# Windowed attention with a gated feed-forward: a third buffer for the turned probabilities, doubled high parts of q and k in DRAM, and a new table of issue points

## The chip, the cores and the metric

The kernel runs on one core of a Trainium2 chip. Times are device microseconds of one execution. The kernel before takes 1642.25 us (median of 3 runs, 1636.55 to 1642.45). TensorE is PE in the profile, its weight load PEld; VectorE is DVE, ScalarE ACT, GpSimd POOL, SyncE SP.

## What is computed

The input x has 2048 rows of 576 numbers.

```python
xn = layernorm(x)
q, k, v = split(xn @ wqkv)                    # 32 heads of 18
mask = (i - j >= 0) & (i - j < 256)           # sliding window
p = softmax(where(mask, q @ k.T * 18**-0.5, -1e9))
s = (p @ v) @ wo
g = silu(((xn @ w_gate) * (xn @ w_up)) @ w_down)   # 576 -> 4608 -> 576
out = x + s * g
```

## The kernel before

**Numbers.** Most operands are a pair of fp16 numbers, a high part and the rest times a constant (the low part); a product runs as passes high by high, high by low and low by high.

**The prologue** (to about 183 us) normalizes x, turns it, and computes v, q and k in two halves of 1024 rows. Each finished tile of q and k (tile `qp`, high part and low part) is stored to `qk_d` in DRAM by `qk_store` (L395). At its end the weights and inputs of the first up-projection are prepared (`sx`, `tf`, `tw`: sums and differences that the seven-product scheme needs).

**Slots.** Then come 72 slots. Slot 4g + c handles the g-th group of 2 x 128 feed-forward columns (18 groups) for the c-th 512 rows. A slot has 16 places. In each place PE gets some matmuls of the up-projection (L1151, 92 of 256 columns in a slot, and L1104, eight with half the rows, four of them at place 6), and everything else is put at a place: `at(slot, place, f)` runs `f` there. A place of 16 or more lies in the next slot. The table `AT` holds the places. Engines execute in order, so a place fixes an instruction's position in the queue of its engine and not its time. SP issues all DMAs in the order of the program, and a DMA that must wait holds those behind it.

**Feed-forward in a slot.** The up results are read out of PSUM by ACT (L1117) and DVE (L1121) into `gt`. The product of gate and up (`ht`, L1126, `seven_mult`) runs on POOL for the first 128 columns and on DVE for the others. `h_hi` (L994, ACT) makes the high part `hh`, `h_lo` (L999, DVE) the low part, and the down-projection (L1015) uses both in the next slot, in five pieces; DVE adds each into `acc` (L1022). In slot 3 of each group of four (3 modulo 4) and slot 0 of the next the weights for the next group are scaled and split: L184 on ACT, L187 on DVE, sums and differences L492 on POOL, `dnw` for the down-projection, whose third part is made on POOL by L592.

**Attention in slots 1 to 64.** One step handles two heads and 512 queries, as four blocks of 128 queries, i0 to i3. A step: scores (L889), masked maxima (L900, DVE), the maxima's scaling (L908, ACT), exponential and its high part (L912, L915, ACT), the low part (L921, POOL or DVE, into `pp`), one transposing DMA for each block (`pt<-pp`, L924), the product with v (`weigh`, L933, 48 matmuls in a step), and the division and store (L945, L946, L953, L960, L961, L970). Table row `p` holds the places of score, shift, exponential, turn and weigh for each block and head. The loads of k, q and v for the next step are L862, L869 and L876. `pt` has two buffers: a block's transpose can start when the block two before it has been weighed.

**The end.** In slots 68 to 70 WO is loaded, its maximum taken (`wo_amax`, through DRAM and back into all partitions, `sd_wo` and `spread`), and scaled (`wo_scale`, L1219, and `wo_split`). From about 1580 us the output projection runs (L1254).

Of the kernel before, what the change touches and what calls it, by code (L numbers as in the profile page):

```python
# [20 lines left out]
def kernel(  # L21
# [23 lines left out]
    scale = DH ** -0.5  # L45
# [14 lines left out]
    G_SC, U_SC, LO = 2.0 ** -23, 2.0 ** -13, 2.0 ** 11  # L60
# [4 lines left out]
    C_OUT = 1.0 / (XS * PROJ * WTOP * WTOP)  # L65
    LEAST, MOST = 2.0 ** -60, 2.0 ** 60

    AT = {"amax": (18, 18, 12),
           "dn": ((43, 42), (53, 57), (57, 54)),
           "down": (6, 8, 11, 14, 17),  # L70
           "end": (28, 30, 33),
           "eng": (0, 1, 0, 0, 0, 0, 0, 0, 0, 0, 1, 0, 0, 0),
           "g0": (-25, -25, -18, -5, -33, -14, -12, -10, -2),
           "h": ((15, 17), (18, 19)),
           "load": (3, 8, 10),
           "mult": {1: 3, 4: 8, 5: 1, 6: 1},
# [6 lines left out]
           "pairs": (6, 13),  # L83
           "raw": (8, 13, 15, 16, -3, -1),
           "scale": (20, 25, 35, 39),
           "sum": ((30, 36, 42, 60, 63), (38, 43, 50, 60, 62)),
# [5 lines left out]
           "t_hi": ((57, 58), (66, 69)),  # L92
           "t_lo": ((58, 59), (70, 70)),
           "u0": ((-9, -8, -5, -5), (-6, -8, -5, -3)),
           "up_hi": (37, 38, 63, 60),
           "up_lo": (42, 40, 65, 62),
           "wd": ((58, 46), (65, 65), (67, 66)),
           "wd0": ((-3, -8), (-1, -2), (-1, 7))}
# [8 lines left out]
    pro = pro_stack.enter_context(tc.tile_pool(name="pro", bufs=1))  # L107
    norm = norm_stack.enter_context(tc.tile_pool(name="norm", bufs=1, side="right"))

    qk_d = dram.tile([2, 2 * D, S], F16, name="qk_d")  # L110
    v_d = dram.tile([S, H * VW], F16, name="v_d")
    o_d = [dram.tile([512, 2 * D], F16, name=f"o_d{i}") for i in range(NCH)]

# [2 lines left out]
    XT2 = const.tile([128, S], F16, name="XT2")  # L116
# [226 lines left out]
    UW, DW, RAW, HT, GT, SC = {}, {}, {}, {}, {}, {}  # L343
# [112 lines left out]

    TF, TW, SX, XD = {}, {}, {}, {}
# [50 lines left out]
    def s_steps(c):  # L510
# [46 lines left out]
        s, m = OP.add, OP.subtract  # L557
# [55 lines left out]
    def at(slot, place, f, *a):  # L613
        todo.setdefault(slot * 16 + place, []).append((f, a))
# [53 lines left out]
    a, b = TB.pop(0)  # L668
# [94 lines left out]
    for t in range(16):  # L763
# [35 lines left out]
        for m in range(QM):  # L799
            for c in (2 * half, 2 * half + 1):  # L800
                qk_tile(UW["q", m], m, c)
                if m == 0:
                    n0 = max(128, c * 512)
# [44 lines left out]
                            fill=-3e38, base=0, channel_multiplier=1)  # L848
    QS, KS, VT, SP, SM, PP, PT, PVB, OB, O3, MX, SMT, RC = {}, {}, {}, {}, {}, {}, {}, {}, {}, {}, {}, {}, {}

    def unit(u, r1, n0, n1):
        return qk_d[0:r1 // DH, u * DH:(u + 1) * DH, n0:n1]


    def load_k(s):
        c, u = s // 16, 2 * (s % 16) + H
        k0 = max(0, c * 512 - 256)
        n = (c + 1) * 512 - k0
        KS[s] = att.tile([128, 768], F16, name="ks", bufs=2)
        for j in range(2):  # L860
            for a, r1 in ((0, 36), (36, 18)):
                nc.sync.dma_start(KS[s][64 * j + a:64 * j + a + r1, 768 - n:], unit(u + j, r1, k0, k0 + n))  # L862
# [55 lines left out]
    def turn_probs(s, j, i):  # L918
        sm, mx, n = SM.pop((s, j, i))
        pp, a = PP[s, i], n * j  # L920
        (nc.gpsimd, nc.vector)[AT["eng"][6 + 2 * i + j]].tensor_tensor(pp[:, a + 2 * n:a + 3 * n], sm, pp[:, a:a + n], op=OP.subtract)  # L921
        if j == 1:
            pt = PT[s, i] = att.tile([128, 12, 128], F16, name="pt", bufs=2)
            nc.sync.dma_start(pt[:, 0:4 * n // 128], PP.pop((s, i))[:, 0:4 * n], transpose=True)  # L924

    def weigh(s, j, i):
# [64 lines left out]

    def h_hi(sl, ft):
        h, hh = HT[sl, ft], h_ring()
        nc.scalar.activation(hh[:, 0], h, AF.Copy, scale=1.0 / LO)  # L994
        HT[sl, ft] = (h, hh)

    def h_lo(sl, ft):
        h, hh = HT[sl, ft]
        nc.vector.scalar_tensor_tensor(hh[:, 1], hh[:, 0], -LO, h, op0=OP.mult, op1=OP.add)  # L999
# [121 lines left out]
        nc.vector.scalar_tensor_tensor(seven_new(sl, name), CH[q], H_SC, x, op0=OP.mult, op1=OP.add)  # L1121

    def seven_mult(sl, f, eng):
        HT[sl, f] = f_ring("ht")
        u = SV.pop((sl, f)).rearrange("p i (k n) -> p k i n", k=2)
        eng.tensor_tensor(HT[sl, f].rearrange("p (i n) -> p i n", i=2), u[:, 0], u[:, 1], op=OP.mult)  # L1126
# [190 lines left out]
```

## Time and profile before

| | |
|---|---|
| median of 3 runs | 1642.25 us |
| the profiled execution, its own time | 1647.93 us |
| its span in the profile | 1646.2 us |
| PE, DVE, ACT, POOL busy | 96%, 77%, 64%, 53% |
| granted TensorE clock, mean | 0.992 |
| DMA moved | 206.91 MB, mean 126 GB/s |

The profiled execution is 0.35% over the median. Its span is 1.73 us shorter than its own time; that rest lies outside the instructions. In the rows, "x<-y" is what an instruction writes and reads, a bracket at the end of a timeline row is the time its engine sat idle before it and what ended that, and "SPq" is SP's queue of DMA issues.

### The profile page before, as it was taken

The numbers are of one execution on the slowest core, as the hardware profiler recorded it, in microseconds if no ns is written. First come the engines' busy times: TensorE is split into PE (matmuls) and PEld (weight loads), VectorE is DVE, ScalarE is ACT, GpSimd is POOL, SyncE is SP. The second block draws the span as 40 slices with busy tenths as digits, with TensorE's granted clock in tenths as the row PEclk, the third lists the DMA queues.
The fourth block names the chain that finished last, engine by engine and source line by source line (L and its number), as shares of the span: only waits on it lengthen the run. The fifth ranks groups of instructions, "written<-read, shape, count | busy, mean of one in ns | idle before, by whom it ended". The sixth has DMA issues, their size and how long they took to land.

```text
span 1646.2 us, 40284 instructions
## 1 busy us (share of the span) xinstructions
PE 1576.6 (96%) x15498; PEld 1106.7 (67%) x15498; DVE 1261.2 (77%) x2752; ACT 1060.2 (64%) x1817; POOL 875.5 (53%) x1100
## 2 busy tenths in 40 slices
PE   8999899999999999999999999999999999999899
PEld 5464576776767666767676667676767666677567
DVE  7536787878788878888878788887878788867555
ACT  6443576777767777777867687777777768752130
POOL 3125565747565656656565657575757475742000
PEclk9999999999999999999999999999999999999999
DMA  9572346565657777676767677777777777751228
GB/s 237 164 194 88 116 83 130 103 123 99 123 107 133 137 119 143 119 147 117 147 107 147 104 146 115 141 123 132 128 138 126 129 123 140 120 95 37 60 67 222
DMA packets 565744, 206.91 MB, mean 126 GB/s; under 512 B 506288, under 2 KB 546352, under 8 KB 565552
## 3 DMA queue, kind: packets, MB, share of 16 engines
q1 hardware_dynamic: 565552, 204.35, 63.8%
q8 instruction: 121, 1.98, 0.5%
q14 instruction: 71, 0.58, 0.1%
HBM read 76.63 MB, written 23.75 MB: 61 GB/s over the span
## 4 chain that ended last, share of the span: by engine, by line
PE 47%; DMA 11%; DVE 11%; POOL 9%; issue 9%; ACT 7%; SPq 5%; ACTq 0%; POOLq 0%; DVEq 0%
PE up L1151 20%; PE dn L1015 10%; DMA pt<-pp 7%; POOL pp L921 4%; PE s L375 3%; PE s L1015 2%; ACT pp L915 2%; PE pv L933 2%; PE s L1254 2%; SPq L924 2%; DVE upw L187 2%; DVE acc L1022 2%; PE up L1254 1%; PE up L1104 1%; PE up L375 1%
## 5 line engine op out<-in xcount | busy, mean ns | idle before, releaser
L1015 PE MATMUL dn<-dnw,hh 128*128 128x512 f16 (+1 forms) x3168 | 447.3, 286 | 9.3 <-DVE hh L999 7.2
L1151 PEld LDWEIGHTS <-tw 128*128 128x128 f16 x3456 | 317.7, 98 | 64.1 <-issue 10.2
L1015 PEld LDWEIGHTS <-hh 128*128 128x128 f16 x3456 | 222.1, 98 | 191.1 <-DVE hh L999 29.8
L1151 PEld LDWEIGHTS <-upw 128*128 128x128 f16 x3024 | 285.0, 98 | 81.9 <-issue 35.2
L1121 DVE SCALAR_TENSOR_TENSOR gt<-up,gt 128x512 f32<-128x512 f32 x360 | 247.0, 686 | 99.3 <-PE up L1104 82.7
L1022 DVE SCALAR_TENSOR_TENSOR acc<-dn,sc,acc 128x512 f32<-128x512 f32 x310 | 214.8, 693 | 112.3 <-PE dn L1015 110.5
L908 ACT ACTIVATE mx<-mx,sig 128x2 f32<-128x2 f32 x256 | 98.2, 383 | 270.3 <-DVE mx L900 270.2
L1151 PE MATMUL up<-XT,upw 128*128 128x256 f16 x2016 | 253.7, 272 | 10.4 <-ACT gt L1117 10.4
L1151 PE MATMUL up<-XT,tw 128*128 128x256 f16 x1728 | 229.4, 277 | 5.9 <-DVE gt L1121 5.9
L1151 PE MATMUL up<-sx,tw 128*128 128x256 f16 x1728 | 231.4, 273 | 2.6 <-ACT gt L1117 1.4
L933 PEld LDWEIGHTS <-pt 128*128 128x128 f16 x2880 | 115.7, 96 | 67.5 <-DMA pt<-pp 45.0
L994 ACT ACTIVATE hh<-ht 128x512 f16<-128x512 f32 x144 | 90.2, 626 | 93.4 <-POOL ht L1126 72.2
L933 PE MATMUL pv<-vt,pt 128*128 128x37 f16 x2880 | 123.4, 179 | 24.8 <-DMA pt<-pp 24.6
L1126 POOL TENSOR_TENSOR ht<-gt 128x512 f32<-128x512 f32 x72 | 92.1, 1279 | 73.2 <-DVE gt L1121 73.1
L1151 PE MATMUL up<-sx,upw 128*128 128x256 f16 x864 | 119.0, 274 | 0.0
L999 DVE SCALAR_TENSOR_TENSOR hh<-hh,ht 128x512 f16<-128x512 f16 x144 | 99.5, 710 | 1.1
L1117 ACT ACTIVATE gt<-up 128x512 f32<-128x512 f32 x144 | 83.8, 582 | 25.4 <-PE up L1104 16.1
L492 POOL TENSOR_TENSOR tf<-raw 128x256 f32<-128x256 f32 x102 | 82.1, 805 | 3.9 <-DVE sc L432 3.3
L187 DVE SCALAR_TENSOR_TENSOR upw<-raw,sc,upw 128x640 f16<-128x640 f32 x72 | 75.1, 1043 | 0.4 <-ACT upw L184 0.4
L1126 DVE TENSOR_TENSOR ht<-gt 128x512 f32<-128x512 f32 x72 | 74.6, 1036 | 0.2
L303 ACT ACTIVATE upw<-raw 128x1280 bf16<-128x1280 f32 (+1 forms) x51 | 62.8, 1232 | 12.0 <-DMA raw<-in_B_w_up_dram 11.5
L187 DVE SCALAR_TENSOR_TENSOR tw<-tf,sc,tw 128x512 f16<-128x512 f32 x68 | 52.9, 799 | 15.7 <-ACT tw L184 15.7
(1354 smaller groups left out, 2842.0 us busy)
## 6 DMA issues: line engine op xcount, KB each, us to landing
raw<-in_B_w_down_dram SPq DMA_DIRECT2D x36, 288.0 KB
qk_d<-qp SPq DMA_DIRECT2D x18, 512.0 KB
raw<-in_B_w_gate_dram SPq DMA_DIRECT2D x36, 256.0 KB
raw<-in_B_w_up_dram SPq DMA_DIRECT2D x36, 256.0 KB
vt<-v_d SPq DMA_DIRECT2D x48, 111.0 KB
ks<-qk_d SPq DMA_DIRECT2D x96, 54.0 KB
v_d<-vo SPq DMA_DIRECT2D x16, 296.0 KB
xr<-in_A_x_dram SPq DMA_DIRECT2D x16, 288.0 KB
```

The costliest lines, as they stand in the source:

```text
L187: nc.vector.scalar_tensor_tensor(w, rv, s, h, op0=OP.mult, op1=OP.subtract)
L492: nc.gpsimd.tensor_tensor(t[:, to], x0, x1, op=OP.subtract)
L908: nc.scalar.activation(mx[:, 1], mx[:, 0], AF.Identity, bias=sig[:, 2:3], scale=sig[:, 1:2])
L933: nc.tensor.matmul(PVB[s][:, j, i, :VW], pt[:, nb * j + n + n // nb * nb], VT[s][:, lo_ + n % nb, j * VW:(j + 1) * VW], start=n == 0, stop ...
L994: nc.scalar.activation(hh[:, 0], h, AF.Copy, scale=1.0 / LO)
L999: nc.vector.scalar_tensor_tensor(hh[:, 1], hh[:, 0], -LO, h, op0=OP.mult, op1=OP.add)
L1015: nc.tensor.matmul(to, a, b, start=q == 0, stop=q == len(l) - 1)
L1022: nc.vector.scalar_tensor_tensor(d, src, SC[g][:, 9:10], d, op0=OP.mult, op1=OP.add)
L1117: nc.scalar.activation(seven_new(sl, name), CH[q], AF.Copy, scale=H_SC)
L1121: nc.vector.scalar_tensor_tensor(seven_new(sl, name), CH[q], H_SC, x, op0=OP.mult, op1=OP.add)
L1126: eng.tensor_tensor(HT[sl, f].rearrange("p (i n) -> p i n", i=2), u[:, 0], u[:, 1], op=OP.mult)
L1151: nc.tensor.matmul(CH[q][:, o], a, b, start=CH["first"], stop=last and q not in (1, 2, 5), skip_group_check=q in ON)
```

## The change

It has these parts.

1. `pt` gets a third buffer. The places of turning and weighing move: the blocks are weighed at 22, 22 to 23, 26 and 28 in place of 18 to 20, 22, 25 and 27. The loads of k, q and v move from places 3, 8, 10 to 7, 10, 14.
2. `qk_d` has four planes in place of two: high, high, low, high. A store of q or k therefore takes one more DMA (two for tile 4, which holds rows of both), and a load of a head takes one DMA of 54 rows in place of two of 36 and 18.
3. The product of gate and up for the second 128 columns is written over its first operand, and one buffer holds that of the first. It is issued one place earlier; the low parts (`h_lo`) move from 18 and 19 to 20 and 21.
4. The split tail weights get a tile `wd` of their own; `xd` takes the place they had in `XT2`.
5. `eng[4]`: the third part of `dnw` is made on ACT in place of POOL.
6. WO: the maxima two places earlier, the transfer out two places earlier, its return one place later, `wo_scale` from place 0 to 6 of slot 70, the splits six places later.
7. Nearly all other places of the table move by some places, also those of the prologue's sums, of which some change between POOL and DVE.

```diff
     AT = {...
-           "eng": (0, 1, 0, 0, 0, 0, 0, 0, 0, 0, 1, 0, 0, 0),
-           "h": ((15, 17), (18, 19)),
-           "load": (3, 8, 10),
-           "p": ((6, 7, 8, 11, 18), (6, 7, 8, 11, 20), (7, 9, 10, 12, 22), (7, 9, 10, 12, 22),
-                 (13, 14, 15, 18, 25), (13, 14, 15, 19, 25), (15, 17, 18, 20, 27), (15, 17, 18, 20, 27)),
+           "eng": (0, 1, 1, 1, 1, 0, 0, 0, 0, 0, 1, 0, 0, 0),
+           "h": ((15, 17), (20, 21)),
+           "load": (7, 10, 14),
+           "p": ((6, 7, 8, 11, 22), (6, 7, 8, 12, 22), (7, 8, 10, 13, 22), (7, 9, 10, 13, 23),
+                 (13, 14, 15, 18, 26), (13, 14, 15, 19, 26), (13, 15, 20, 21, 28), (15, 17, 20, 21, 28)),
...
-    qk_d = dram.tile([2, 2 * D, S], F16, name="qk_d")
+    qk_d = dram.tile([4, 2 * D, S], F16, name="qk_d")
...
-    def f_ring(name):
-        return post.tile([128, 512], F32, name=name, bufs=4 if name == "gt" else 2)
...
-        nc.sync.dma_start(qk_d[:, m * 128:(m + 1) * 128, hs].rearrange("k r n -> r k n"), q)
+        rs = slice(m * 128, (m + 1) * 128)
+        nc.sync.dma_start(qk_d[1:3, rs, hs].rearrange("k r n -> r k n"), q)
+        for part in (0,) if m < 4 else (0, 3) if m == 4 else (3,):
+            nc.sync.dma_start(qk_d[part, rs, hs], q[:, 0])
...
     def wd_part(g, kind, i):
-        o = 1024 * (g % 2) + 512 * i + 128 * kind
-        return XT2[:, o:o + 128]
+        if g not in WD:
+            WD[g] = ring.tile([128, 2, 2, 128], F16, name="wd", bufs=1)
+        return WD[g][:, i, kind]
...
-            XD[c] = sums.tile([128, 256], F16, name=f"xd{c}")
+            XD[c] = XT2[:, 512 * c:512 * c + 256]
...
-    def unit(u, r1, n0, n1):
-        return qk_d[0:r1 // DH, u * DH:(u + 1) * DH, n0:n1]
+    def unit(u, part, n0, n1):
+        return qk_d[part:part + 3, u * DH:(u + 1) * DH, n0:n1]
...
-            for a, r1 in ((0, 36), (36, 18)):
-                nc.sync.dma_start(KS[s][64 * j + a:64 * j + a + r1, 768 - n:], unit(u + j, r1, k0, k0 + n))
+            nc.sync.dma_start(KS[s][64 * j:64 * j + 54, 768 - n:], unit(u + j, 1, k0, k0 + n))
...
-            pt = PT[s, i] = att.tile([128, 12, 128], F16, name="pt", bufs=2)
+            pt = PT[s, i] = att.tile([128, 12, 128], F16, name="pt", bufs=3)
...
-        HT[sl, f] = f_ring("ht")
         u = SV.pop((sl, f)).rearrange("p i (k n) -> p k i n", k=2)
-        eng.tensor_tensor(HT[sl, f].rearrange("p (i n) -> p i n", i=2), u[:, 0], u[:, 1], op=OP.mult)
+        HT[sl, f] = u[:, 0] if f else post.tile([128, 512], F32, name="ht", bufs=1).rearrange("p (i n) -> p i n", i=2)
+        eng.tensor_tensor(HT[sl, f], u[:, 0], u[:, 1], op=OP.mult)
...
-        at(NSLOT - 4, 2 * k + 14, wo_amax, k)
-        at(NSLOT - 2, 3 * k + 2, wo_split, k)
-    at(NSLOT - 3, 8, wo_out)
-    at(NSLOT - 3, 12, wo_in)
-    at(NSLOT - 2, 0, wo_scale)
+        at(NSLOT - 4, 2 * k + 12, wo_amax, k)
+        at(NSLOT - 2, 3 * k + 8, wo_split, k)
+    at(NSLOT - 3, 6, wo_out)
+    at(NSLOT - 3, 13, wo_in)
+    at(NSLOT - 2, 6, wo_scale)
```

Three places of the order show what the table does. The first is SP's queue from the end of slot 49 to slot 50, before: `vt`, `ks` and `qs` are loads for attention, `o_d` is a store of its result, and the four transposes are those of one step, i0 and i1 in the first row of them, then i2, then i3.

```order
L876 DMA vt<-v_d 128x6x74
L924 DMA_TRANSPOSE pt<-pp 128x12x128 x2
L970 DMA o_d_81<-ob 128x4x72
L970 DMA o_d_81<-ob 128x4x8
L924 DMA_TRANSPOSE pt<-pp 128x12x128
L862 DMA ks<-qk_d 36x1x768
L862 DMA ks<-qk_d 18x768
L862 DMA ks<-qk_d 36x1x768
L862 DMA ks<-qk_d 18x768
L924 DMA_TRANSPOSE pt<-pp 128x12x128
```

And the same part of SP's queue in the changed kernel:

```order
L923 DMA_TRANSPOSE pt<-pp 128x12x128 x2
L875 DMA vt<-v_d 128x6x74
L969 DMA o_d_81<-ob 128x4x72
L923 DMA_TRANSPOSE pt<-pp 128x12x128
L969 DMA o_d_81<-ob 128x4x8
L923 DMA_TRANSPOSE pt<-pp 128x12x128
L969 DMA o_d_81<-ob 128x4x64
L862 DMA ks<-qk_d 54x1x768 x2
L868 DMA qs<-qk_d 54x1x512 x2
```

The loads of `ks` have moved from between the transposes of i2 and i3 to behind both, and are two in place of four.

The second is POOL's queue at the end of slot 51 (3 modulo 4), before: L492 makes sums for the next group's weights, L953 to L961 finish an attention step, L1126 is the product of gate and up that ACT waits for.

```order
L921 TENSOR_TENSOR pp<-sm__18782,pp 128x384 x2
L492 TENSOR_TENSOR tf<-raw_17807,tf 128x256
L492 TENSOR_TENSOR tf<-raw_17953,tf 128x256
L953 TENSOR_TENSOR o_18885<-o_18885,rc 128x144
L960 CAST ob<-o_18885 128x4x36
L961 TENSOR_TENSOR ob<-o_18885,ob 128x4x36
L492 TENSOR_TENSOR tf<-raw_17953 128x256
L1126 TENSOR_TENSOR ht<-gt_18642 128x512
```

In the changed kernel:

```order
L920 TENSOR_TENSOR pp<-sm__18552,pp 128x384 x2
L493 TENSOR_TENSOR tf<-raw_17641,tf 128x256
L493 TENSOR_TENSOR tf<-raw_17641 128x256
L1126 TENSOR_TENSOR ht<-gt_18415 128x512
L952 TENSOR_TENSOR o_18655<-o_18655,rc 128x144
L959 CAST ob<-o_18655 128x4x36
L960 TENSOR_TENSOR ob<-o_18655,ob 128x4x36
```

The product now stands ahead of the three instructions that finish the attention step and behind one sum less.

The third is DVE's queue from the end of slot 69 into slot 70, before: L1219 to L163 are `wo_scale`, which waits for the `spread` transfer, and behind it stand the second product L1126 and the low parts L999 that the down-projection needs.

```order
L1121 SCALAR_TENSOR_TENSOR gt_24299<-up,gt_24299 128x512
L1219 TENSOR_REDUCE ps_o<-spread 128x1
L159 TENSOR_SCALAR ps_o<-ps_o 128x1
L161 TENSOR_SCALAR ps_o<-ps_o 128x1
L162 RECIPROCAL ps_o<-ps_o 128x1
L163 TENSOR_SCALAR ps_o<-ps_o 128x1
L1126 TENSOR_TENSOR ht<-gt_24299 128x512
L1022 SCALAR_TENSOR_TENSOR acc<-s,sc,acc 128x4x64
L999 SCALAR_TENSOR_TENSOR hh<-hh,ht 128x512
```

In the changed kernel:

```order
L1121 SCALAR_TENSOR_TENSOR gt_24009<-up,gt_24009 128x512
L1126 TENSOR_TENSOR gt_24009<-gt_24009 128x2x256
L1022 SCALAR_TENSOR_TENSOR acc<-s,sc,acc 128x4x64
L999 SCALAR_TENSOR_TENSOR hh<-hh,ht 128x512
L999 SCALAR_TENSOR_TENSOR hh<-hh,gt_24009 128x512
L1121 SCALAR_TENSOR_TENSOR gt_24193<-up,gt_24128 128x512
L1022 SCALAR_TENSOR_TENSOR acc<-s,sc,acc 128x512
L1219 TENSOR_REDUCE ps_o<-spread 128x1
```

Both low parts and the product now stand ahead of `wo_scale`.

More of the change, by code (lines that the diff above doesn't have):

```diff
@@ L66 @@
     LEAST, MOST = 2.0 ** -60, 2.0 ** 60
-    AT = {"amax": (18, 18, 12),
-           "dn": ((43, 42), (53, 57), (57, 54)),
+    AT = {"amax": (21, 21, 11),
+           "dn": ((44, 44), (53, 54), (52, 52)),
            "down": (6, 8, 11, 14, 17),
-           "end": (28, 30, 33),
-           "eng": (0, 1, 0, 0, 0, 0, 0, 0, 0, 0, 1, 0, 0, 0),
-           "g0": (-25, -25, -18, -5, -33, -14, -12, -10, -2),
-           "h": ((15, 17), (18, 19)),
-           "load": (3, 8, 10),
-           "mult": {1: 3, 4: 8, 5: 1, 6: 1},
[6 rows of a table removed]
+           "end": (28, 31, 35),
+           "eng": (0, 1, 1, 1, 1, 0, 0, 0, 0, 0, 1, 0, 0, 0),
+           "g0": (-21, -19, -19, -16, -30, -17, -12, -10, -7),
+           "h": ((15, 17), (20, 21)),
+           "load": (7, 10, 14),
+           "mult": {1: 11, 4: 10, 5: 1, 6: 0},
[6 rows of a table added]
            "pairs": (6, 13),
-           "raw": (8, 13, 15, 16, -3, -1),
-           "scale": (20, 25, 35, 39),
-           "sum": ((30, 36, 42, 60, 63), (38, 43, 50, 60, 62)),
+           "raw": (6, 8, 11, 13, -9, -6),
+           "scale": (22, 26, 35, 44),
+           "sum": ((29, 33, 48, 59, 66), (38, 53, 56, 61, 62)),
            "sx": ((-24, -24, -24, -23, -22, -22, -18, -18, -18, -17, -14, -13, -13, -14, -10, -10, -9),
[4 rows of a table removed]
[L92 to L98, printed above, removed]
[4 rows of a table added]
+           "t_hi": ((57, 58), (67, 69)),
+           "t_lo": ((58, 60), (70, 71)),
+           "u0": ((-8, -8, -7, -6), (-6, -8, -7, -4)),
+           "up_hi": (36, 39, 60, 59),
+           "up_lo": (41, 41, 66, 61),
+           "wd": ((55, 48), (63, 70), (67, 74)),
+           "wd0": ((-4, -8), (-1, 3), (-1, 8))}
     ctx.enter_context(tc.manual_schedule())
@@ L454, in up_lo @@
            w[:, 0:5])
-    TF, TW, SX, XD = {}, {}, {}, {}
+    TF, TW, SX, XD, WD = {}, {}, {}, {}, {}
     def wd_part(g, kind, i):
-        o = 1024 * (g % 2) + 512 * i + 128 * kind
-        return XT2[:, o:o + 128]
+        if g not in WD:
+            WD[g] = ring.tile([128, 2, 2, 128], F16, name="wd", bufs=1)
+        return WD[g][:, i, kind]
     def wd_sum(g, kind):
@@ L867, in load_q @@
         for j in range(2):
-            for a, r1 in ((0, 18), (18, 36)):
-                nc.sync.dma_start(QS[s][64 * j + a:64 * j + a + r1], unit(u + j, r1, c * 512, (c + 1) * 512))
+            nc.sync.dma_start(QS[s][64 * j:64 * j + 54], unit(u + j, 0, c * 512, (c + 1) * 512))
     def load_v(s):
@@ L993, in h_hi @@
         h, hh = HT[sl, ft], h_ring()
-        nc.scalar.activation(hh[:, 0], h, AF.Copy, scale=1.0 / LO)
+        nc.scalar.activation(hh[:, 0].rearrange("p (i n) -> p i n", i=2), h, AF.Copy, scale=1.0 / LO)
         HT[sl, ft] = (h, hh)
@@ L998, in h_lo @@
         h, hh = HT[sl, ft]
-        nc.vector.scalar_tensor_tensor(hh[:, 1], hh[:, 0], -LO, h, op0=OP.mult, op1=OP.add)
+        a, b = (hh[:, k].rearrange("p (i n) -> p i n", i=2) for k in range(2))
+        nc.vector.scalar_tensor_tensor(b, a, -LO, h, op0=OP.mult, op1=OP.add)
         HT[sl, ft] = hh
```

16 rows, old and new, of the table AT are left out of this document.

## The prediction

> **What bounds the kernel now.** I read the page first.
>
> ```profile
> span 1646.2 us, 40284 instructions
> PE 1576.6 (96%) x15498; PEld 1106.7 (67%) x15498; DVE 1261.2 (77%) x2752; ACT 1060.2 (64%) x1817; POOL 875.5 (53%) x1100
> PE 47%; DMA 11%; DVE 11%; POOL 9%; issue 9%; ACT 7%; SPq 5%; ACTq 0%; POOLq 0%; DVEq 0%
> ```
>
> PE is busy 96% of the span and idle 69.6 us. The change removes no matmul, so the gain can only come from idle time and from stretches in which PE is slow. The chain goes through DMA, DVE, POOL and ACT for 38%, so these set the pace in places. To find where, I take 48 whole slots, from place 6 of slot 17 to place 6 of slot 65; the half-row matmuls L1104 mark them in PE's timeline. The third and fourth row mark a slot in which nothing waits.
>
> ```profile
> 499.14 0.39 PE L1104 MATMUL up<-XT,upw 64*128 64x256 f16 x4
> 1399.48 0.39 PE L1104 MATMUL up<-XT,upw 64*128 64x256 f16 x4
> 1418.13 0.39 PE L1104 MATMUL up<-XT,upw 64*128 64x256 f16 x4
> 1457.77 0.39 PE L1104 MATMUL up<-XT,upw 64*128 64x256 f16 x4
> ```
>
> An undisturbed slot takes 18.65 us, so 48 would take 895.2. They take 958.6. The excess is **63.4 us**, the most that the change can win here. The busy-time windows and PE's waits of that stretch split it (waited in all, times, longest).
>
> ```profile
> 499.10:1457.80 958.70, 916.63 (x9792) 655.53 (x9792) 780.67 (x1728) 706.00 (x1178) 602.39 (x732) 0.99 0.74 130
> PE pv L933 <- DMA pt<-pp: 24.6, 26, 2.3
> PE up L1151 <- ACT gt L1117: 11.8, 13, 1.4
> PE dn L1015 <- DVE hh L999: 3.4, 12, 0.3
> PE dn L1015 <- DVE acc L1022: 2.1, 12, 0.2
> ```
>
> PE idles 42.1 us, of which the four waits are 41.9. The other 21.3 us of the excess passes while PE counts as busy. PE's timeline in slots 48 and 50, with the clock of one window, shows what that is.
>
> ```profile
> 1126.95 0.47 PE L933 MATMUL pv<-vt,pt 128*128 128x37 f16 x12 [1.97 <-DMA pt<-pp]
> 1127.26 1.76 PE L1151 MATMUL up<-XT,tw 128*128 128x256 f16 x12
> 1127.00:1131.00 4.00, 4.00 (x37) 2.44 (x38) 1.50 (x4) 0.00 (x0) 2.06 (x5) 0.66 0.96 206
> 1167.00 1.47 PE L1151 MATMUL up<-XT,tw 128*128 128x256 f16 x12
> ```
>
> After a wait of 1.97 us the granted clock is 0.66 for 4 us and twelve matmuls take 1.76 us, not 1.47. A long wait is thus paid again, 0.34 x 4.0 = 1.4 us. (The Trainium skill, "TensorE: Matmul & The Clock Gate", section "Why this matters for your kernels", sees throughput drop for PE-idle gaps over about 3 us. This trace differs: 1.97 us of idle stands right before the low clock. By that rule the slow stretches have another cause and stay; it is a rival below.) I share the 21.3 us among the waits by their idle time: 24.6 / 41.9 of it, 12.5 us, goes with the transposes. They cost **37.1 us**, the rest **26.3**.
>
> **Part 1, the transposes.** SP's timeline around the stall in slot 53, the wait at its end on PE, and a row of SP's waits:
>
> ```profile
> 1216.15 1.97 SPq L924 DMA_TRANSPOSE pt<-pp  x1
> 1218.16 2.33 SPq L862 DMA_DIRECT2D ks<-qk_d  x4
> 1220.66 2.14 SPq L924 DMA_TRANSPOSE pt<-pp  x1
> 1227.06 0.51 PE L933 MATMUL pv<-vt,pt 128*128 128x37 f16 x12 [2.02 <-DMA pt<-pp]
> SPq L924 <- PE pv L933: 31.8, 42, 1.7
> ```
>
> The first is block i2, the second i3. i3 stands behind i2, behind 2.33 us of k loads, and needs the buffer that i1 leaves; its issue ends at 1222.80 and PE can go on at 1227.06, 4.26 us later. The change takes both away: the k loads go behind i3 (and are two, so about 1.17 us of SP time), and a third buffer means that i2 needs none that this step uses and i3 only that of i0. Weighing moves later by one place for i2 and i3 (18.65 / 16 = 1.17 us) and two to four for i0, which frees nothing early but is not needed early either. In slot 53 i3 is issued 2.33 us sooner without the loads, and PE asks 1.17 later: 3.50 us against a wait of 2.02. The longest wait of all is 2.3. What could stay is the transpose that `pp` itself delays, since i3 is also turned one place later (1.17): then the margin is 2.33 against 2.3 and some remain. **Bounds**: if only the place counts, each of 26 waits (mean 0.95) loses up to 1.17, and only those over it keep a rest: by 2.3 - 1.17 at most 1.1 each, for perhaps a third of them 10 us of wait and its slow clock, so a gain of 22; with everything removed 37. I take **32**, nearer the upper end because two causes go at once.
>
> **Parts 3 and 5 and the table, slots 3 to 0 modulo 4.** The rest, 26.3 us, lies in 12 changes of group, 2.2 each. Around one of them, on POOL, ACT and PE:
>
> ```profile
> 1193.23 1.27 POOL L1126 TENSOR_TENSOR ht<-gt 128x512 f32<-128x512 f32 x1
> 1193.26 0.82 ACT L184 ACTIVATE upw<-raw,sc 128x640 f16<-128x640 f32 x1
> 1194.54 0.63 ACT L994 ACTIVATE hh<-ht 128x512 f16<-128x512 f32 x1 [0.45 <-POOL ht L1126]
> 1195.71 0.60 PE L1151 MATMUL up<-XT,upw 128*128 128x256 f16 x4 [0.95 <-ACT gt L1117]
> ```
>
> PE waits for ACT's reading L1117, which stands behind L994, which waits for the product on POOL. In the new order the product stands ahead of the finish of the attention step (L953 to L961), and ACT's weight split of 0.82 is issued earlier, with one of a quarter of that width in its place. 0.45 + about 0.4 us goes, of 0.95. But DVE has no room there:
>
> ```profile
> 1187.70:1205.90 18.20, 16.79 (x173) 11.65 (x170) 17.92 (x38) 13.94 (x26) 12.65 (x15) 1.00 0.72 141
> ```
>
> DVE (the third pair) is busy 17.92 of 18.20 us. Once ACT is in time, PE waits for DVE a little further on, at L999 or L1022, unless DVE has less to do. The split rows of the weights stay in number; some of them (one of 0.35 us, and a split of the down weights) move out of this stretch, but one maximum (L900) is issued ahead of the low parts that was behind them. I count about 0.75 us less for DVE ahead of what PE needs, and half of the 26.3 as gained: **13**, with bounds 5 (DVE takes all of what ACT gives back, and only the 3.4 + 2.1 goes) and 20 (about 1.7 a group). Moving a third of the down weights from POOL to ACT costs ACT this much:
>
> ```profile
> L592 POOL TENSOR_SCALAR dnw<-dnw 128x576 f16<-128x576 f16 x36 | 59.7, 1673 | 0.7 <-ACT dnw L184 0.7
> L184 ACT ACTIVATE dnw<-raw,sc 128x576 f16<-128x576 f32 x36 | 26.0, 767 | 0.0
> ```
>
> No row shows the operation on ACT; the nearest of its size is 767 ns, so 36 x 0.77 = 28 us for ACT, from 0 to 28 on the path. ACT is busy 64% and waits most of all for DVE's maxima, which covers it: 0. POOL gets 59.7 us back in the same stretch. The later low parts (places 20, 21) cost nothing while DVE has room ahead of place 6, as it has in the other slots:
>
> ```profile
> 1137.16 1.29 DVE L999 SCALAR_TENSOR_TENSOR hh<-hh,ht 128x512 f16<-128x512 f16 x2
> 1139.87 0.69 DVE L1121 SCALAR_TENSOR_TENSOR gt<-up,gt 128x512 f32<-128x512 f32 x1 [1.42 <-PE up L1104]
> ```
>
> Between the low parts' end at 1138.45 and the next reading DVE idles 1.42 us. Writing the product over its operand and reading it with a stride are new; no row has them. The operand's buffer is now held to place 21 and written again at place 22, both on DVE in that order, so 0.
>
> **Slots 0 to 15.** PE's wait for the low parts in that stretch, four times:
>
> ```profile
> PE dn L1015 <- DVE hh L999: 3.7, 4, 0.9
> ```
>
> Transposes are not waited for there. The same shortening of DVE by 0.75 at four group changes would give 3.0, and 3.7 with some restart of PE is all that there is: **2.5**, between 0 and 5.
>
> **The start of slot 0.** PE's first long wait, DVE's queue ahead of what ends it, and the windows:
>
> ```profile
> 188.84 1.44 PE L1151 MATMUL up<-XT,tw 128*128 128x256 f16 x6 [5.18 <-DVE gt L1121]
> 187.49 0.69 DVE L532 TENSOR_TENSOR tf<-tf,XT 128x512 f32<-128x512 f32 x1
> 186.00:196.00 10.00, 7.16 (x48) 5.18 (x47) 8.35 (x14) 3.32 (x7) 3.64 (x3) 0.66 0.50 150
> ```
>
> DVE is late with the first L1121 behind sums of inputs and weights. In the new order two sums L532 fewer stand ahead of it, 2 x 0.69 = 1.4 us. The clock of 0.66 over the 10 us behind the wait costs 3.4; in proportion, 1.4 / 5.18 of it, 0.9 goes too: **2.3**, from 0 (if another sum is late instead) to 5.2.
>
> **Part 6, slot 70.** DVE's row, and PE's two waits behind it:
>
> ```profile
> 1544.80 0.29 DVE L1219 TENSOR_REDUCE ps_o<-spread 128x1 f32<-128x128 f32 x1 [6.45 <-DMA spread<-sd_wo]
> 1547.49 0.86 PE L1015 MATMUL s<-dnw,hh 128*128 128x512 f16 x3 [3.95 <-DVE hh L999]
> 1549.28 0.61 PE L1015 MATMUL s<-dnw,hh 128*128 128x512 f16 x1 [0.92 <-DVE hh L999]
> ```
>
> DVE stands 6.45 us at `wo_scale`, and the low parts behind it make PE wait 3.95 + 0.92 = 4.9. In the new order they are ahead of it, `wo_scale` comes six places later (about 6.3 us in these shorter slots) and its transfer starts earlier. The wait has no place left: 4.9, with 1.4 of slow clock and some of the slow start behind it **6.5**, from 4 to 8.5.
>
> **Part 2, the stores and loads.** The extra DMAs come in the prologue.
>
> ```profile
> qk_d<-qp SPq DMA_DIRECT2D x18, 512.0 KB
> 69.00:81.00 12.00, 12.00 (x60) 5.14 (x59) 7.95 (x26) 6.07 (x11) 2.85 (x4) 1.00 1.02 263
> 105.00:115.00 10.00, 10.00 (x84) 7.99 (x82) 0.50 (x2) 3.46 (x8) 0.00 (x0) 1.00 1.12 220
> ```
>
> There are 20 more stores of half a pair, 256 KB: 5.2 MB, at 263 GB/s 20 us of all 16 DMA engines, half of it in each half. The engines are full in these two windows (DMA share over 1) while PE has no gap in them, and have room between them. I take **-2**, from 0 (all in gaps) to -10 (one half's share in full). Loads of q and k are halved in number, not in bytes; their gain is in part 1. Part 4 changes names of memory only: 0.
>
> **Sum.** 32 + 13 + 2.5 + 2.3 + 6.5 - 2 = 54.3 us. Against the profiled execution's own 1647.93 (1.73 of it outside the span, which stays) this gives 1593.6. That execution lies 5.7 us over the median of 1642.25, so from the median it would be 1588. I take **1590**, between the two.
>
> **Rivals.**
> 1. *DVE becomes the bound.* The group changes gain only 5 and slots 0 to 15 nothing: 1600. For it: 17.92 of 18.20 us. Against: less work is ahead.
> 2. *Transposes stay late.* `pp` delays them and not the buffer: 22 in place of 32 at the best, 10 at the worst, and with rival 1 on top the sum is 54 - 22 - 8 - 2.5 = 22: 1620. For it: i3 is turned a place later. Against: SP waited 31.8 us for PE to leave a buffer, and 2.33 us of loads are gone in any case.
> 3. *The slow clock stays* whatever the waits do. The clock's own share of the 48 slots is (1 - 0.99) x 958.7 = 9.6 us, so 1600. For it: the DMA engines are busy 0.96 in the slow window, which could be another cause. Against: the window begins with a wait. (It is what the Trainium skill's rule, cited above, would give.)
> 4. *The low parts come too late for the down-projection in every slot*, since they are issued two places (2.3 us) later and DVE had 1.42 us of room there. If L999 lands behind what PE needs by t, 71 slots pay it: from t = 54 / 71 = 0.76 us on the kernel is slower than before. A wait of 0.9, the longest in slots 0 to 15 above, costs 64 us, so 1652. Against: the low parts are needed at place 8 only, some two places behind.
> 5. *The table does not do what its places say*, because engines run behind their places: the sum of parts 1 and 3 falls away and 10 to 15 us of the ends remain, 1630.
>
> **How the numbers follow.** Chances: forecast (1578 to 1600) 0.50, rivals 1 and 3 0.18 together, rival 2 0.15, rival 5 0.08, rival 4 0.07, and 0.02 for more than all bounds. A measurement of this kernel tells about 0.5% from no change, so 8.2 us. Faster by more than that holds for all but rival 4 and a part of rival 5: 0.87; same 0.06; slower 0.07. The range takes the forecast with its bounds, rivals 1 and 3 and most of rival 2: the lower end is the sum with every upper bound (37 + 20 + 5 + 5.2 + 8.5 = 76, 1642 - 76 = 1566, taken as 1570), the upper 1622.
>
> **What would show it.** Part 1: PE's wait for `pt<-pp` falls from 24.6 to under 5 us and the low-clock windows inside slots 16 to 64 go. The group changes: PE's wait for ACT's L1117 goes, and the slots 0 modulo 4 show what DVE leaves. Slot 70: no DVE wait for `spread` and no PE wait there. The start: PE's 5.18 shrinks to about 3. The stores: PE gets idle time before 183 us, or slot 0 starts later. The forecast is wrong if PE waits for L999 in slots other than 0 modulo 4, or if transposes are still waited for by more than 10 us.

## The result and the profile after

The changed kernel takes 1582.34 us (median of 4 runs, 1581.73 to 1582.93); the kernel before took 1640.45 in the runs beside it. The ratio is 0.9649, with a 95% interval from 0.9627 to 0.9670: 3.5% faster, 58.1 us. Profile against profile it is 65 us, since the profiled execution of before (1647.93, clock 0.992) is longer than all its others on record (1642.45 at most; clock 0.993 to 0.996 where it is on record), and that of after is an ordinary one (1582.93, span 1581.0). One execution of the kernel before, beside the first group of experiments, took 7337.3 us and is left out of every figure here.

The head of the page of the changed kernel, with the chain that ended last:

```profile
span 1581.0 us, 40009 instructions
PE 1557.1 (98%) x15498; PEld 1108.4 (70%) x15498; DVE 1255.7 (79%) x2755; ACT 1070.1 (68%) x1853; POOL 831.7 (53%) x1061
PE 80%; DVE 9%; ACT 3%; issue 3%; POOL 2%; DMA 2%; SPq 0%; ACTq 0%; DVEq 0%; POOLq 0%
```

The chain now runs through PE for 80%, 47% before, and DMA has gone from 11% to 2%. PE's timeline at the same marks as before (L1104 at place 6 of slots 0, 1, 17 and 65):

```profile
184.63 0.39 PE L1104 MATMUL up<-XT,upw 64*128 64x256 f16 x4
200.42 0.39 PE L1104 MATMUL up<-XT,upw 64*128 64x256 f16 x4
491.92 0.39 PE L1104 MATMUL up<-XT,upw 64*128 64x256 f16 x4
1400.56 0.39 PE L1104 MATMUL up<-XT,upw 64*128 64x256 f16 x4
```

And in the kernel before, slots 0 and 1, which the prediction does not show:

```profile
183.26 0.39 PE L1104 MATMUL up<-XT,upw 64*128 64x256 f16 x4
201.44 0.39 PE L1104 MATMUL up<-XT,upw 64*128 64x256 f16 x4
```

The 48 slots take 908.6 us, not 958.6: 50.0 less. Slots 0 to 16 take 307.3, not 315.9: 8.6 less, of which slot 0 by itself (15.8 in place of 18.2) is 2.4. From slot 65 to the end it is 180.4, not 188.4: 8.0 less. The prologue is 1.4 longer. Together 65.2.

The busy-time window of the 48 slots and all of PE's waits there, then its waits from slot 0 to slot 17:

```profile
491.90:1400.50 908.60, 902.08 (x9781) 657.09 (x9780) 778.71 (x1728) 711.32 (x1202) 578.84 (x708) 1.00 0.74 137
PE up L1104 <- DVE upw L185: 6.3, 12, 0.5
PE up L1151 <- DVE gt L1121: 3.6, 2, 3.2
```

The four waits of before, for the transposes, for ACT's L1117, for L999 and for L1022, are gone from the list. One new wait stands there: in the 12 slots 0 modulo 4, PE waits at the half rows (L1104) for a split of the up weights on DVE. The clock is 1.00. In slot 0 the first wait is still 3.2 us.

### The profile page after: what moved, and what is told of

Its sections match the earlier page's. It is cut to its first block, busy times and chain, and to the rows that moved or that the text cites. A ratio compares the mean times of both kernels' runs of the same rounds, so it can differ in the third digit from the quotient of the medians.

```text
span 1581.0 us, 40009 instructions
## 1 busy us (share of the span) xinstructions
PE 1557.1 (98%) x15498; PEld 1108.4 (70%) x15498; DVE 1255.7 (79%) x2755; ACT 1070.1 (68%) x1853; POOL 831.7 (53%) x1061
## 3 DMA queue, kind: packets, MB, share of 16 engines
q1 hardware_dynamic: 566384, 209.58, 65.2%
## 4 chain that ended last, share of the span: by engine, by line
PE 80%; DVE 9%; ACT 3%; issue 3%; POOL 2%; DMA 2%; SPq 0%; ACTq 0%; DVEq 0%; POOLq 0%
PE up L1151 37%; PE dn L1015 21%; PE s L373 4%; PE pv L932 4%; PE up L1104 3%; PE s L888 2%; PE s L1015 2%; DVE upw L185 2%; PE s L1254 2%; PE up L1254 2%; PE up L373 1%; PE s L324 1%; DVE gt L1121 1%; DVE pp L920 1%; DVE acc L1022 1%
## 5 line engine op out<-in xcount | busy, mean ns | idle before, releaser
L1151 PEld LDWEIGHTS <-upw 128*128 128x128 f16 x3024 | 289.9, 98 | 70.0 <-issue 22.2
L1121 DVE SCALAR_TENSOR_TENSOR gt<-up,gt 128x512 f32<-128x512 f32 x360 | 247.3, 687 | 73.9 <-PE up L1104 56.8
L1022 DVE SCALAR_TENSOR_TENSOR acc<-dn,sc,acc 128x512 f32<-128x512 f32 x310 | 215.1, 694 | 92.9 <-PE dn L1015 91.4
L1151 PE MATMUL up<-XT,upw 128*128 128x256 f16 x2160 | 259.5, 273 | 0.0
L1151 PE MATMUL up<-XT,tw 128*128 128x256 f16 x1728 | 243.7, 272 | 4.2 <-DVE gt L1121 3.9
L1151 PE MATMUL up<-sx,tw 128*128 128x256 f16 x1728 | 223.3, 273 | 0.0
L1126 POOL TENSOR_TENSOR ht<-gt 128x512 f32<-128x512 f32 x72 | 99.6, 1384 | 91.2 <-DVE gt L1121 86.0
L932 PEld LDWEIGHTS <-pt 128*128 128x128 f16 x2880 | 110.1, 96 | 17.8
L932 PE MATMUL pv<-vt,pt 128*128 128x37 f16 x2880 | 112.8, 179 | 0.0
L1117 ACT ACTIVATE gt<-up 128x512 f32<-128x512 f32 x144 | 83.2, 578 | 19.2 <-PE up L1104 10.9
L993 ACT ACTIVATE hh<-ht 128x512 f16<-128x512 f32 x72 | 44.9, 623 | 56.2 <-POOL ht L1126 56.2
L1104 PE MATMUL up<-XT,upw 64*128 64x256 f16 x432 | 59.5, 274 | 6.3 <-DVE upw L185 6.3
L493 POOL TENSOR_TENSOR tf<-raw,tf 128x256 f32<-128x256 f32 x68 | 49.4, 726 | 28.4 <-DVE tw L185 28.4
```

Source lines behind the costliest of these rows:

```text
L493: nc.gpsimd.tensor_tensor(t[:, to], x0, x1, op=OP.subtract)
L932: nc.tensor.matmul(PVB[s][:, j, i, :VW], pt[:, nb * j + n + n // nb * nb], VT[s][:, lo_ + n % nb, j * VW:(j + 1) * VW], start=n == 0, stop ...
L1022: nc.vector.scalar_tensor_tensor(d, src, SC[g][:, 9:10], d, op0=OP.mult, op1=OP.add)
L1104: nc.tensor.matmul(CH[q][:, 256 * kind:256 * kind + 256], w, x, start=False, stop=s and kind == 1, skip_group_check=q in ON)
L1117: nc.scalar.activation(seven_new(sl, name), CH[q], AF.Copy, scale=H_SC)
L1126: eng.tensor_tensor(HT[sl, f], u[:, 0], u[:, 1], op=OP.mult)
```

## The experiments

The changed kernel is the reference of most of them. Each stands with its median; the runs of the kernel before beside them had the medians 1635.5, 1635.8 and 1636.6 in the three groups.

**1. The third buffer taken away, all else as changed.**

```diff
-            pt = PT[s, i] = att.tile([128, 12, 128], F16, name="pt", bufs=3)
+            pt = PT[s, i] = att.tile([128, 12, 128], F16, name="pt", bufs=2)
```

> The changed kernel with two buffers for P turned. Theory A (the buffer is needed where the weighing stands now): block i2 cannot be turned before i0 is weighed at place 22, so it lands at about place 26 and i3 at about 28 to 29; PE waits for the transposes by 0.3 to 1.5 us in most of 48 slots, 20 to 60 us with the slow clock, time 1600 to 1640. Theory B (the later asking and the order of the loads did it, the buffer little): wait for the transposes under 5 us, time 1580 to 1588.

1622.9 us, ratio to before 0.991 (0.9874 to 0.9946). PE's wait, and SP's wait ahead of a transpose for the product with v, of this run and then of the changed kernel:

```profile
PE pv L932 <- DMA pt<-pp: 34.0, 62, 2.2
SPq L923 <- PE pv L932: 209.0, 64, 4.4
```

```profile
SPq L923 <- PE pv L932: 93.7, 62, 2.6
```

Theory A: under the new places the buffer is worth 40.6 us. By the table the new places ask for it: blocks i0 and i1 are weighed later and hold their buffers longer, and SP's wait for PE to leave one is 209.0 us here. Even with three buffers SP waits longer for PE than before (93.7 us, 31.8 before); it just no longer reaches PE.

**2. Blocks i2 and i3 weighed at 25 and 27 again.**

```diff
-                 (13, 14, 15, 18, 26), (13, 14, 15, 19, 26), (13, 15, 20, 21, 28), (15, 17, 20, 21, 28)),
+                 (13, 14, 15, 18, 25), (13, 14, 15, 19, 25), (13, 15, 20, 21, 27), (15, 17, 20, 21, 27)),
```

> The changed kernel, but blocks i2 and i3 are weighed at 25 and 27 as before; three buffers, the loads behind the transposes. Theory B: i3 landed at place 27.16 in the median in the changed kernel, so PE waits some 0.2 to 0.9 us for it in most of 48 slots, 10 to 35 us, time 1592 to 1617. Theory A (the buffer and the loads alone suffice): under 5 us of wait, time 1580 to 1588.

1580.4 us, and of PE's waits for a transpose one of 0.3 us is left in the stretch from 480 to 1440 us. Asking later was not needed for the gain. The expectation compared a landing at place 27.16 with the start of place 27; but in the program a place begins with up matmuls and a piece of the down-projection, and the weighing stands behind them, so the room was larger than I counted.

**3. The loads of k, q and v at their old places.**

```diff
-           "load": (7, 10, 14),
+           "load": (3, 8, 10),
```

> The changed kernel with the loads of k, q and v at places 3, 8, 10 again, one load for a head still. If the k loads between the transposes of i2 and i3 were what made i3 late: i3 lands up to one place later, at 27.5 to 28.3, and PE waits 0 to 0.4 us in a slot, up to 20 us, time 1583 to 1603. If they are hidden by the buffer that i3 waits for: within 3 us of the changed kernel, 1580 to 1586.

1583.4 us (1581.6 and 1585.3); PE's wait for the transposes is 0.9 us in 2 places. With three buffers, and one load for a head, where the loads stand matters no more.

**4. All the new code under the old table of places** (and WO's five lines as before).

```diff
-    AT = {...the new places
+    AT = {...the old places
```

> The changed code (three buffers, doubled high parts with one load for each, product written over its operand, tile for the tail weights) under the whole old table of places. If the code does the main part: PE's wait for the transposes falls from 24.6 to under 8 us, time 1605 to 1618 (the group changes, slot 70 and slot 0 keep their waits). If the table does it: wait for the transposes over 15 us, time 1628 to 1645.

1619.8 us, ratio 0.989 (0.9856 to 0.9923). PE's waits in the stretch from 490 to 1440 us:

```profile
PE up L1151 <- ACT gt L1117: 11.1, 12, 1.3
PE pv L932 <- DMA pt<-pp: 5.0, 8, 1.0
PE dn L1015 <- DVE hh L999: 3.4, 12, 0.3
PE dn L1015 <- DVE acc L1022: 2.1, 12, 0.2
```

The code takes the wait for the transposes from 24.6 to 5.0 us under the old places; the other three rows stand as before to within 0.7 us. So the waits at the changes of group, and those in slots 0 and 70, go with the table and WO's lines. The time is 1.8 us over the range that was expected. The third buffer and the halved loads are both in this run, so it does not tell which of the two does it; the buffer alone under the old places was not run.

**5. In the kernel before, only the loads moved** (the second suspect of part 1 by itself).

```diff
-           "load": (3, 8, 10),
+           "load": (7, 10, 14),
```

> The kernel before with only the places of the loads of k, q and v moved to 7, 10, 14, so that no load stands between the transposes of i2 and i3; two buffers, old planes, old places else. If the k loads ahead of i3 are a second cause beside the buffer, as predicted: PE's wait for the transposes falls from 24.6 to under 10 us, time 1612 to 1625. If the buffer alone holds i3: wait 18 to 26 us, time within 6 us of before.

1628.6 us, ratio 0.9937 (0.9914 to 0.9959). PE's waits from 495 to 1450 us, and ACT's wait for the raw up weights in this run and before:

```profile
PE up L1151 <- ACT gt L1117: 18.2, 21, 1.5
PE dn L1015 <- DVE hh L999: 3.4, 12, 0.3
PE pv L933 <- DMA pt<-pp: 3.4, 8, 1.3
```

```profile
ACT upw L303 <- DMA raw<-in_B_w_up_dram: 29.2, 14, 3.5
```

```profile
ACT upw L303 <- DMA raw<-in_B_w_up_dram: 11.5, 11, 3.2
```

The wait for the transposes falls from 24.6 to 3.4 with two buffers: moving the loads is enough to cure it, and so is the new code with the loads at their old places (run 4). But the loads now stand ahead of the raw weights in SP's queue, ACT waits for those, and behind ACT's maximum stands L1117. SP's timeline from slot 52 to 53 shows the order; the second row is two transposes:

```profile
1194.68 2.31 SPq L869 DMA_DIRECT2D qs<-qk_d  x4
1197.15 4.81 SPq L924 DMA_TRANSPOSE pt<-pp  x2
...
1205.00 0.58 SPq L179 DMA_DIRECT2D raw<-in_B_w_up_dram  x1
1205.62 0.48 SPq L181 DMA_DIRECT2D raw<-in_B_w_up_dram  x1
```

And ACT's timeline of the same run waits for them in slot 53:

```profile
1209.46 1.27 ACT L303 ACTIVATE upw<-raw 128x1280 bf16<-128x1280 f32 x1 [2.59 <-DMA raw<-in_B_w_up_dram]
1210.64 0.19 ACT L303 ACTIVATION_READ_ACCUMULATOR upw<-raw 128x1 f32 x1
1210.73 0.58 ACT L1117 ACTIVATE gt<-up 128x512 f32<-128x512 f32 x1
```

This gives back a part: the 48 slots are 23.5 us shorter than in the profile of before, with L1117 waited for by 6.4 us more, and slots 0 to 16 are 4.0 longer. The time missed the expected range, 1612 to 1625; between the medians the gain is 8.0 us. The new table also moves the raw loads, from places 8, 13, 15, 16 to 6, 8, 11, 13.

**6. Two planes for q and k again**, without the extra stores and with two loads for a head, at the new places.

```diff
-    qk_d = dram.tile([4, 2 * D, S], F16, name="qk_d")
+    qk_d = dram.tile([2, 2 * D, S], F16, name="qk_d")
...
-        for part in (0,) if m < 4 else (0, 3) if m == 4 else (3,):
-            nc.sync.dma_start(qk_d[part, rs, hs], q[:, 0])
...
+            for a, r1 in ((0, 36), (36, 18)):
+                nc.sync.dma_start(KS[s][64 * j + a:64 * j + a + r1, 768 - n:], unit(u + j, r1, k0, k0 + n))
```

> The changed kernel with q and k in two planes again: no extra stores, two loads for a head, at the new places 7 and 10. If the doubled planes pay through the loads: SP issues four loads each, 2.3 us more in a slot, and transposes are waited for again, 5 to 15 us, time 1587 to 1597. If they only cost their stores: slot 0 starts 1 to 2 us sooner, time 1579 to 1583.

1586.2 us in two runs (1584.7 and 1587.8). PE waits for transposes 1.8 us and for ACT's L1117 1.2 us again between 480 and 1440 us. It is between the two theories: the doubled planes seem to be worth some 4 us at the new places, and two runs do not settle the size. With three buffers the loads that are not halved bring little of the wait back.

**7. The third part of the down weights on POOL again.**

```diff
-           "eng": (0, 1, 1, 1, 1, 0, 0, 0, 0, 0, 1, 0, 0, 0),
+           "eng": (0, 1, 1, 1, 0, 0, 0, 0, 0, 0, 1, 0, 0, 0),
```

> The changed kernel with the third part of the down weights on POOL again (36 instructions of 1.67 us). If moving it to ACT helped: POOL is late with the low parts of P or with the product in slot 3 modulo 4, 0.5 to 1.2 us in 17 groups, time 1590 to 1603. If it is hidden on either engine: 1580 to 1585.

1582.8 us: hidden on either engine.

**8. The old lines on WO.**

```diff
-        at(NSLOT - 4, 2 * k + 12, wo_amax, k)
-        at(NSLOT - 2, 3 * k + 8, wo_split, k)
-    at(NSLOT - 3, 6, wo_out)
-    at(NSLOT - 3, 13, wo_in)
-    at(NSLOT - 2, 6, wo_scale)
+        at(NSLOT - 4, 2 * k + 14, wo_amax, k)
+        at(NSLOT - 2, 3 * k + 2, wo_split, k)
+    at(NSLOT - 3, 8, wo_out)
+    at(NSLOT - 3, 12, wo_in)
+    at(NSLOT - 2, 0, wo_scale)
```

> The changed kernel with the five lines on WO as before (maxima, transfer, wo_scale at place 0 of slot 70). If the wait at wo_scale is what slot 70 lost: PE waits there again 4.9 us, with the slow clock 6.5 to 8.5, time 1588 to 1591. If the earlier product and low parts had already freed it: under 2 us, 1581 to 1584.

1587.2 us, 4.9 more. PE's timeline in slot 70 of this run, one wait where there were two:

```profile
1490.10 1.89 PE L1015 MATMUL s<-dnw,hh 128*128 128x512 f16 x4 [3.40 <-DVE hh L999]
```

**9. One split of the up weights earlier on DVE,** against the new wait.

```diff
-           "up_lo": (41, 41, 66, 61),
+           "up_lo": (41, 41, 65, 61),
```

> The changed kernel with one split of the up weights on DVE (L185) one place earlier in slots 0 modulo 4, ahead of a low part of P (L920) and not behind it. In the changed kernel PE waits there 0.8 us at L1104 in 12 slots. If only the order on DVE is at fault: 7 to 9.6 us less, time 1573 to 1576. If DVE is simply full: the wait goes to L999 or L1022 a little further on, time 1580 to 1584.

1581.9 us. PE's wait at L1104 is gone, and in its place stands, from 480 to 1440 us:

```profile
PE dn L1015 <- DVE hh L999: 7.9, 12, 0.7
```

DVE is full there (17.78 of 18.20 us, from 1143.66 to 1161.86), and what is issued first only decides who waits.

**10. POOL's three instructions that finish an attention step ahead of the product again.**

```diff
-           "end": (28, 31, 35),
+           "end": (28, 30, 35),
```

> The changed kernel with POOL's three instructions that finish an attention step ahead of the product of gate and up again (1.5 us in slot 3 modulo 4). If the order on POOL is what took the wait for L1117 away: PE waits for ACT there again by 0.3 to 1.0 us in 12 groups, time 1585 to 1594. If DVE sets the pace of that stretch: the ACT wait only takes the place of part of the 0.8 us at L1104, time 1581 to 1584.

1581.1 us. PE waits 4.0 us for ACT's L1117 in 12 places, and its wait at L1104 falls out of the list, so the sum stays. The order on POOL, on which I had put a part of the gain, is not needed for it while DVE is behind.

**11. One low part of P from DVE to POOL** (block i2, first head).

```diff
-           "eng": (0, 1, 1, 1, 1, 0, 0, 0, 0, 0, 1, 0, 0, 0),
+           "eng": (0, 1, 1, 1, 1, 0, 0, 0, 0, 0, 0, 0, 0, 0),
```

> The changed kernel with the low part of P for block i2 of the first head on POOL and not on DVE (L920, 0.5 to 1.1 us in each slot). If DVE is full from slot 3 to slot 0 modulo 4 and that is all that is left there: the 0.8 us in 12 slots and the 0.2 at L1022 go, 7 to 12 us, time 1570 to 1575; i2 is turned 0.7 to 1.2 us later, within its room of three places. If POOL becomes late instead: PE waits for the transposes or for ACT, 1580 to 1595.

1582.9 us, and neither cause that was expected: the wait is again at L999, 6.8 us in 12 slots, though DVE has one instruction less, and PE waits neither for ACT nor for transposes by more than 0.3 us. DVE's timeline in that stretch of the changed kernel, and then of this run:

```profile
1151.80 1.09 DVE L920 TENSOR_TENSOR pp<-sm__18689,pp 128x384 f16<-128x384 f32 x1
1152.82 1.53 DVE L185 SCALAR_TENSOR_TENSOR upw<-raw,sc,upw 128x640 f16<-128x640 f32 x1
1154.38 0.35 DVE L185 SCALAR_TENSOR_TENSOR wd<-raw,sc,wd 64x128 f16<-64x128 f32 x1
1154.76 0.69 DVE L999 SCALAR_TENSOR_TENSOR hh<-hh,ht 128x512 f16<-128x512 f16 x1
```

```profile
1150.82 1.55 DVE L185 SCALAR_TENSOR_TENSOR upw<-raw,sc,upw 128x640 f16<-128x640 f32 x1
1152.40 0.70 DVE L185 SCALAR_TENSOR_TENSOR wd<-raw,sc,wd 64x128 f16<-64x128 f32 x1
1153.13 1.29 DVE L999 SCALAR_TENSOR_TENSOR hh<-hh,ht 128x512 f16<-128x512 f16 x1
```

The instruction of 1.09 us is gone, and two of the next three have become longer, 0.35 to 0.70 and 0.69 to 1.29: 0.95 us. POOL's timeline of this run says what runs beside them:

```profile
1151.64 1.31 POOL L493 TENSOR_TENSOR tf<-raw 128x256 f32<-128x256 f32 x1
1152.91 0.96 POOL L920 TENSOR_TENSOR pp<-sm__18689,pp 128x384 f16<-128x384 f32 x1
```

**12. Both, the last edit and nine sums of slot 0 moved six places later** (`sx` for the third 512 rows).

```diff
-                  (-13, -11, -10, -9, -7, -7, -3, -1, 2, 3, 4, 5, 6, 4, 6, 7, 12),
+                  (-13, -11, -10, -9, -7, -7, -3, -1, 8, 9, 10, 11, 12, 10, 12, 13, 18),
```

> As the run before, and the sums for the third 512 rows that DVE makes at places 2 to 12 of slot 0 moved to places 8 to 18. PE's first wait in slot 0 (3.4 us for L1121, with a slower clock behind it) should fall under 0.5 us, 3 to 6 us beside the gain of the run before: 1566 to 1571. If later sums hold DVE in the same slot: within 2 us of the run before.

1586.7 us (1585.6 to 1587.1), 4.3 us slower than the changed kernel. PE's waits in slot 0 and the next (183 to 215 us):

```profile
PE up L1151 <- ACT gt L1117: 2.7, 1, 2.7
PE up L1151 <- DVE gt L1121: 2.3, 4, 0.8
PE up L1104 <- DVE gt L1121: 1.6, 1, 1.6
```

The wait of 3.2 us at L1121 is split into smaller ones, and these add up to more than it; the moved sums hold up what stands behind them. No version beat the changed kernel by more than 2 us.

## Why the prediction was right, and where its steps were not

The sum of 54.3 us stands against 65.0 between the profiled executions (1647.93 to 1582.93), and 1590 against 1582.34. Its terms, with the marks above:

| term | predicted | measured |
|---|---|---|
| transposes, 48 slots | 32 | about 36.5 |
| changes of group, 48 slots | 13 | about 13.5 |
| slot 0 | 2.3 | 2.4 |
| slots 1 to 16 | 2.5 | 6.2 |
| slot 65 to the end | 6.5 | 8.0 |
| stores | -2 | -1.4 |

The two rows of the 48 slots are split by changes of group in which PE waits for no transpose, such as slots 51 and 52 of the kernel before:

```profile
1177.57 0.39 PE L1104 MATMUL up<-XT,upw 64*128 64x256 f16 x4
1197.48 0.39 PE L1104 MATMUL up<-XT,upw 64*128 64x256 f16 x4
1217.11 0.39 PE L1104 MATMUL up<-XT,upw 64*128 64x256 f16 x4
```

They take 39.5 us, 2.24 over two undisturbed slots; twelve such changes make 26.9 of the excess of 63.4, and 36.5 is left for the transposes. After, the whole excess is 13.4, all of it at the changes of group. So the split 37.1 to 26.3, which the prediction took by shares of idle time, was right to 1 us.

The measured column belongs to the long profiled execution of before. Run 4's profile, which agrees with it to 1.4 us in each of the prologue, slots 0 to 16 and the end, is 27.2 us shorter, while between the medians of that group the new code is worth 15.7. So some 10 us of the transposes' 36.5 may be that execution's own; no trace of a shorter one of before shows it.

**The transposes: the right kind of size, but the causes were not two that add up.** The step held that the k loads and the buffer were late together, "nearer the upper end because two causes go at once". Either edit removes most of the wait by itself: the loads in run 5 (24.6 to 3.4), the new code in run 4 (24.6 to 5.0), and in the changed kernel the later asking (run 2) or the new places of the loads (run 3) can be taken back. That 32 comes near is in part luck: the step added 2.33 us for the loads and 1.17 for the later asking, and each of the two could be taken back at no cost. The step also held that weighing i0 later "frees nothing early but is not needed early either". It frees late: SP's wait for PE went from 31.8 to 93.7 us, and with two buffers the new places cost 40.6 (run 1). Rival 2, that transposes stay late because of `pp`, is out: SP still waits for `pp`, 90.8 us on DVE and 86.1 on POOL, but PE no longer waits for a transpose.

**The slow clock** went with the waits in the 48 slots (0.99 to 1.00), against rival 3. But it is only a part of the 21.3 us that pass busy. Slot by slot, four of the 48 are under 1.00 before, at 0.92 or 0.93, each with a wait of 1.97 to 2.31 us for a transpose; together they lose about 7 us by it. Run 1 has 62 waits for transposes, two of them over 2 us in the stretch from 490 to 1440 us, and its clock there is 1.00:

```profile
490.00:1440.00 950.00, 920.26 (x9914) 663.42 (x9913) 782.84 (x1750) 720.03 (x1217) 574.33 (x717) 1.00 0.74 133
```

So a wait of 2 us can be followed by a slow clock, as in slot 48 before, and need not be. Yet run 1's 48 slots (501.67 to 1456.91 us) take 46.6 us more than the changed kernel's, with 26.9 us of waits for transposes: a wait costs more than PE's idle time at full clock too. There the step "a long wait is thus paid again" by the clock fails; what the rest is stays open. The Trainium skill's rule ("TensorE: Matmul & The Clock Gate", section "Why this matters for your kernels", no gaps over about 3 us) fits run 1 and not slot 48.

**The changes of group: right that half goes and DVE keeps the rest, wrong where.** The rest is 13.4 us, 1.1 at each of 12 changes, 0.5 of it idle. I expected it at L999 or L1022; it came at L1104, at a split of the up weights that stands behind a low part of P on DVE (the rows in run 11). Runs 9, 10 and 11 agree with rival 1's mechanism at the new level: DVE is full there, the wait goes to L999 or to L1117, and the time stays. That the product moved ahead on POOL is not needed for the time (run 10). So the size was right, but the step that put 0.45 + 0.4 us on the product and ACT's split is not shown; which of the moved pieces brought the gain was not tried one by one, and the cause of these 13.5 us is open.

**Slots 0 to 16.** Slot 0 was sized right. Its first wait went from 5.18 to 3.17 us, and the clock of the window from 186 to 196 us, which lies 1.4 us earlier in the slot after than before, from 0.66 to 0.83:

```profile
188.18 2.19 PE L1151 MATMUL up<-XT,tw 128*128 128x256 f16 x11 [3.17 <-DVE gt L1121]
186.00:196.00 10.00, 7.82 (x57) 5.95 (x57) 9.34 (x15) 3.82 (x7) 4.52 (x4) 0.83 0.55 178
```

The four changes of group behind it were mis-sized, 6.2 in place of 2.5. The waits of up to 0.9 us for L999 there are all gone, and I had bounded the term by their 3.7 us; a change of group costs more than its idle time, as in the 48 slots (2.24 with 1.4 idle in slots 51 and 52).

**WO**: the wait went as the step said; 8.0 against 6.5. Put back alone, the old lines cost 4.9 (run 8): one wait of 3.40 is left, where there were 3.95 and 0.92. That the earlier product and low part took the other is likely, not shown.

**The covers held.** The third part of the down weights takes 0.67 us on ACT, where 0.77 was taken from the nearest row, and is hidden on either engine (run 7):

```profile
L591 ACT ACTIVATE dnw<-dnw 128x576 f16<-128x576 f16 x36 | 22.6, 673 | 0.0
```

The low parts two places later made no slot late (rival 4: PE's list for the 48 slots has no L999). The stores' price of 1.4 us is not told apart from chance: slot 0's mark stood between 182.5 and 184.7 us over the runs with the new stores, and at 183.3, 183.6 and 184.2 in the three traces without them.

## What to carry to other kernels

Before a buffer is added, look at what stands in the queue of the late transfer: here moving the loads (run 5) cured the same wait as the third buffer and the halved loads did (run 4), and what they were moved ahead of then waited in their place. When the work of one engine fills a stretch, changing its order moved the wait to another line and not the end (runs 9 and 10); less work there, and less beside it on an engine that slows it, should help, which no run here tried. Idle time in front of a wait is not its whole cost: an undisturbed period of the loop, held against the disturbed ones, gave more than the sum of the waits.

## What the runs showed of the hardware

POOL slows DVE where both run instructions with two tensor inputs from SBUF. The same split of 128x640 took 0.88 us and 1.53 us in one change of group of the changed kernel, and the low part L999 0.69 us with nothing on POOL and 1.29 us beside POOL (run 11), so that moving one instruction from DVE to POOL gave DVE nothing. In the changed kernel every low part whose row stands alone with POOL idle took 0.68 or 0.69 us, and all those over 0.7, up to 1.41, had a tensor operation of POOL beside them. One row suggests that the delay can fall on POOL too: the split of 0.88 us ran beside POOL's product L1126, and that product took 1.86 us, against 1.38 in the mean. The Trainium skill names it, "GPSIMD Engine Reference", section "8. Key points": POOL shares its SBUF interfaces with VectorE, and they contend when a VectorE instruction has two SBUF inputs; the trace agrees, and gives the price here, 1.7 to 2.0 times in the rows shown.
